# A fused attention and gated-unit kernel: later q loads, one low part on VectorE, and the last stage's attention rows split later

## The chip, the cores and the metric

The kernel runs on one core of one Trainium2 chip. The metric is the device time of one execution in microseconds (us); the time before is the median of three runs. The engines are called as the profile calls them: PE (TensorE; PEld is its weight load), DVE (VectorE), ACT (ScalarE), POOL (GpSimd) and SP (SyncE), which here only issues transfers, in the order of the program.

## The reference

Input x has 2048 rows of 448. Two branches are mixed by a gate of one number a row.

```
g = sigmoid((x * gate_w).sum(-1))
q, k, v = split(x @ wqkv)                  # 16 heads of 28
p = softmax(q @ k.T * 28 ** -0.5)          # per head, 2048 x 2048
a = concat(p @ v) @ wo
gate, up = x @ W_gate, x @ W_up            # 448 x 1792 each
b = (gate * (gate > 0) * up) @ W_down
out = g * a + (1 - g) * b
```

## The kernel before

Products are made at near full precision from split operands. An f32 matrix becomes a high part, an ACT copy rounded to the matmul's format (`act_high`), and a low part, the difference of the two (`low` on DVE, `pool_low` on POOL). A product is a sum of terms over high and low parts.

The program has three stages. The first projects x to q, k and v and writes q and k to DRAM. The second walks through 32 rounds, two per head (v = 2h and 2h + 1). The third is the output stage.

A round's order is written out by hand as a string of letters, one per small step, for all engines at once: `s` is a score block (PE, then ACT), `m` a row-maximum product for two heads ahead (PE, then DVE), `x` one product of the gate-and-up projection, `g` and `e` steps of the softmax, `P` and `Q` the products with v. PE is filled with the gate-and-up products, worked off as 56 units, one for each block of 128 hidden columns (14) and of 512 rows (4). A unit of 22 products reads one weight tile `wg`. Two such tiles exist. When a unit ends, `load_f` (line 588) refills its tile from `ws_d` in DRAM for the unit after next. The hidden block `h` goes to `h_d`, to be read back in the output stage.

In each even round, at its first score, `loads` brings K and q of the head two ahead: K as two transfers (line 167), q as one copy within SBUF (line 172) and four transfers (line 175). At the sixth score `small_things` sends the previous head's row sums to DRAM (`l_d`, line 665, after DVE's reciprocal `rq`) and reads them back spread over partitions (`rb`, line 671, which waits until `l_d` has landed). SP issues all of these in one queue, and whatever waits there holds what stands behind it.

The output stage is a list `todo`. `down(i)` is one of 56 steps of the down projection, 14 for each block of 512 rows, into four accumulators `acc`. Around it stand `fetch_w` and `split_wd` (weights `wdr`, split to `WD`: high on ACT, low on POOL), `fetch_h` and `split_d` (hidden rows `hr`, split to `hh`: high on ACT, low on DVE; three `hh` buffers, so ACT's split for step i + 2 waits for step i - 1). For each row block `fetch_o` loads the attention rows `or`, `split_o` splits them in two halves to `on` (high on ACT, low on POOL), `wout` multiplies a quarter of them by the output weights `WO` in 11 products, the last four with the low parts, and `result` joins both branches. `split_wo` splits the output weights `wor`. A table gives, for each row block, the step before which its load, its two splits and its four output products are put.

Of the kernel before, what the change touches and what calls it, by code (L numbers as in the profile page):

```python
# [84 lines left out]
def gated_mix_kernel(ctx, tc, x, wq, wo, wgu, wd, out):  # L85
# [8 lines left out]
    def f32(ap):  # L94
        return ap.bitcast(F32)
# [21 lines left out]
    def ps_x(name):  # L117
        return psum.tile([P, TB], F32, tag="x", bufs=2, name=name)
# [7 lines left out]
    def low(dst, src, high):  # L126
        nc.vector.tensor_tensor(dst, src, f32(high), op=OP.subtract)  # L127

    def pool_low(dst, src, high):
        nc.gpsimd.tensor_tensor(dst, src, f32(high), op=OP.subtract)  # L130
# [20 lines left out]
    def last_q(name, dt=F32R):  # L151
        return vp.tile([P, 4, TB], dt, name=name, tag="Q2", bufs=1)
# [11 lines left out]
    def load_k(h):  # L164
        k = qk_d[2 * DH * h:2 * DH * h + DH].rearrange("d r t -> (d r) t")
        for a in (0, 2 * DH):
            nc.sync.dma_start(f32(K[h % 3])[a:a + 2 * DH], k)

    def load_q(h):
        Q[h] = QS[h % 3].rearrange("p j t -> p (j t)")  # L170
        if h > 2:
            nc.sync.dma_start(f32(Q[h])[GD:GD + 2], f32(Q[h])[GD + 2:GD + 4])
        for a in range(2):
            for r in range(2):
                nc.sync.dma_start(f32(Q[h])[2 * DH * a + r:2 * DH * (a + 1):2], qk_d[2 * DH * h + DH:2 * DH * (h + 1), a])
# [14 lines left out]
    def smax(k):  # L190

        h, u, half = maxima[k]
        full = 4 * rows_of(h).count(2)
        if u == 0 and half == 0:
            MX[h] = keep.tile([P, 2 * full], F32, name=f"mx_{h}", tag="mx", bufs=2)
            M[h] = keep.tile([P, NU[h]], F32, name=f"m_{h}", tag="m", bufs=2)
        ps = ps_w(f"sm_{k}")
        for c in range(2):
            k0 = (half * 2 + c) * TB
            nc.tensor.matmul(ps[:, c, :], Q[h][:, u * P:(u + 1) * P], K[h % 3][:, k0:k0 + TB],  # L200
                             start=True, stop=True)
        c = 2 * u + half
        to = MX[h][:, c:c + 1] if u < full else M[h][:, u:u + 1]
        nc.vector.tensor_reduce(to, ps, axis=AX.XY, op=OP.max)  # L204
        if c == 2 * full - 1:
            nc.vector.tensor_reduce(M[h][:, :full], MX.pop(h).rearrange("p (a b) -> p a b", b=2), axis=AX.X, op=OP.max)
# [87 lines left out]
    def score():  # L294

        v, done, q, half, chunks = stream.pop(0)
        h = v // 2
        if q not in QUAD:
            QUAD[q] = p_slot(next(slots) % NP, f"P_{v}_{q[1]}_{q[2]}")
        ps = ps_w(f"s_{v}_{chunks[0][0]}_{chunks[0][1]}")  # L300
        for c, (k, j) in enumerate(chunks):
            nc.tensor.matmul(ps[:, c], K[h % 3][:, k * P:(k + 1) * P], Q[h][:, j * TB:(j + 1) * TB], start=True, stop=True)  # L302
            AT[v, k, j] = QUAD[q][:, 2 * half + c]
        dst = QUAD[q][:, 2 * half:2 * half + 2]
        if done:
            nc.scalar.activation(dst, ps, AF.Exp, scale=SCALE)  # L306
        else:
            nc.scalar.activation(dst, ps, AF.Copy, scale=-1.0)  # L308
            todo_max.append((v, chunks[0][1], dst, ps if v else None))
# [275 lines left out]
    def load_f(i):  # L585
        if NF <= i < NB * NF:
            WS[i] = fe.tile([P, 2, 7, P], F32R, name=f"wg_{i}", tag="wg", bufs=2)
            nc.sync.dma_start(f32(WS[i]), ws_d[i % NF])
# [103 lines left out]
    def early_d():  # L692

        for i in range(0, 4, 2):
            h = fe.tile([P, 2, 4, P], F32, name=f"hk_{i}", tag="wgr", bufs=2).rearrange("p s c f -> p (s c f)")
            for k in range(2):
                DR[i + k] = V[:, 0].rearrange("p k h d -> p (k h d)")[:, (i + k) * D:(i + k + 1) * D]
                HK[i + k] = h[:, k * TB:(k + 1) * TB]
                nc.sync.dma_start(DR[i + k], wd[(i + k) * P:(i + k + 1) * P])
                nc.sync.dma_start(HK[i + k], h_d[i + k])  # L700
# [13 lines left out]
    def small_things(u):  # L714

        h, q = divmod(u, 4)

        if u in (22, 38):
            g = 2 if u < 32 else 3
            nc.sync.dma_start(V[:, g % 2], v_d[g])  # L720
        if u == 1:
            gates()
        if u == 2:
            pack_wo()
        if h and q == 1:
            row_sums(h - 1)
            spread(h - 1)

    def loads(h):

        if 2 < h + 2 < H:
            load_k(h + 2)
            load_q(h + 2)

    split_f(0, act_high, pool_low, (0,))
    fetch_f(1)
    for v, order in enumerate(ROUNDS):
        small_things(2 * v)
        if v == 2 * H - 3:
            early_d()  # L740
        ns = 0
        for o in order:
            if o == "s":
                ns += 1
                if ns == 6:
                    small_things(2 * v + 1)
                if ns == 1 and v % 2 == 0:
                    loads(v // 2)
                if stream:
                    score()  # L750
            elif o == "m":
                if m < len(maxima):
                    smax(m)
                    m += 1
            elif o == "x":
                i, half, n = passes.pop(0)
                if n == 0:
                    units.append((i, half, ps_x(f"gu_{i}_{half}")))
                gu_mm(units[-1][2], i, half, n)
                if n == NT - 1:  # L760
                    i, half, ps = units.pop()
                    if half:
                        finished.add(i)
                        load_f(i + 2)
                    spill_h(i, ps) if half else relu(i, ps)
            elif o == "n":
                if v % 2 and v < 2 * H - 1:
                    smax_end(v // 2 + 1)
            elif o == "w":
                ready = -(-starts[v + 2] // NT)  # L770
                ready = min(ready + ready % 2, 2 * NF)
                while parts < ready and (parts < 4 or parts // 2 - 2 in finished):
                    split_f(parts // 2, act_high, pool_low, (parts % 2,))
                    parts += 1
                    if parts % 2 == 0:
                        fetch_f(parts // 2 + 1)
            elif o == "b":
                block_min()
            elif o == "A":
                all_max()  # L780
            elif o == "g":
                take_max()
            elif o == "N":
                if v > 1 and v % 2:
                    normalise(v // 2 - 1)
            elif o == "e":
                take_exp()
            elif o in "cf":
                rescale(v, "cf".index(o))
            elif o == "D":  # L790
                split_wd(len(early))
                early.append(o)
            elif o == "l":
                sends.pop()()
            elif o == "u":
                split_f(0, act_high, pool_low, (1,))
                QS.append(last_q("Q2"))
                for a, b in ((GD, 12), (GD + 12, 4)):
                    nc.sync.dma_start(f32(QS[2])[a:a + b].rearrange("p j t -> p (j t)"), Q[1][GD + 2:GD + 2 + b].bitcast(F32))
                load_q(2)  # L800
                fetch_f(2)
                parts = 2
            elif o in "PQ":
                pv(v, "PQ".index(o))
        rest = [k for k in todo_exp + todo_sub + todo_all if k[0] == v]
        assert not rest and v not in PO or len(stream) == max(0, 16 * (2 * H - 1 - v) - AHEAD), (v, passes, rest, len(stream) + 16 * (v + 1))
# [6 lines left out]
    WO = pf.tile([P, 7, D], F32R, name="WO")  # L813
# [7 lines left out]

    def split_wo(r):
        act_high(WO[:, 0:3], r[:, 0:3])
        pool_low(WO[:, 3:6], r[:, 0:3], WO[:, 0:3])
        act_high(WO[:, 6], r[:, 3])
        pool_low(WO[64:, 6], r[64:, 3], WO[64:, 6])

    ON, OR, GA, HH, ACC = {}, {}, {}, {}, {}

# [105 lines left out]
        todo[n:n] = new  # L935


    for tb, load, split, at in ((0, 3, (5, 6), (9, 10, 11, 12)), (1, 8, (13, 14), (16, 17, 18, 19)), (2, 21, (23, 25), (28,) * 4),
                                (3, 35, (37, 39), (42,) * 4)):
        before(load, (fetch_o, tb))  # L940
        for k, i in enumerate(split):
            before(i, (split_o, tb, 2 * k))
        for t, i in enumerate(at):
            before(i, (wout, tb, t))
# [40 lines left out]
```

## Time and profile before

| | |
|---|---|
| median of three timed runs | 1223.49 us (1223.36 to 1225.96) |
| the profiled execution | 1228.39 us, span 1226.6 us |
| mean granted PE clock | 0.994 |
| busy: PE, DVE, ACT, POOL | 1199.1, 906.3, 867.9, 753.9 us |
| transferred | 178.36 MB, 145 GB/s over the span |

The span runs from the first to the last instruction. The profile names, for each instruction, the idle time of its engine before it and what ended that time. `wg<-ws_d` means that the tile `wg` is written from `ws_d`. The first stage takes some 140 us, the rounds last until about 1030 us, and the rest is the output stage.

### The profile page before, as it was taken

How to read it: one execution, taken by the hardware profiler on the slowest of the kernel's cores; microseconds unless marked ns; L12 is line 12 of the kernel's file. 1: busy time of each engine (PE TensorE's matmuls, PEld its weight loads, DVE VectorE, ACT ScalarE, POOL GpSimd, SP SyncE). 2: the span in 40 equal slices, each digit the busy share in tenths (PEclk: the TensorE clock that was granted, in tenths of full speed). 3: DMA queues.
4: the chain of work that ended last, by engine and by line, in shares of the span. 5: the costliest groups of instructions: out<-in, count | busy, mean ns of one | idle time of the engine just before them, and what ended most of it. 6: DMA issues, size and time to landing. Idle time of an engine off the chain costs nothing.

```text
span 1226.6 us, 16848 instructions
## 1 busy us (share of the span) xinstructions
PE 1199.1 (98%) x6183; PEld 823.1 (67%) x6183; DVE 906.3 (74%) x1177; ACT 867.9 (71%) x956; POOL 753.9 (61%) x328
## 2 busy tenths in 40 slices
PE   9999999999999999999999999999999999899998
PEld 6888655565656565656665666666565656799997
DVE  6466798889898888978897989898888552443342
ACT  5322798998989888877887888888887886422121
POOL 4221588989898766666775777777666885621020
PEclk9999999999999999999999999999999999899999
DMA  9856444454445435152545344354523325633342
GB/s 329 297 197 258 146 161 135 148 168 129 141 124 184 116 143 152 52 155 78 155 134 163 112 121 129 104 143 159 152 81 117 121 86 183 182 122 119 108 134 81
DMA packets 63486, 178.36 MB, mean 145 GB/s; under 512 B 13050, under 2 KB 19650, under 8 KB 58754
## 3 DMA queue, kind: packets, MB, share of 16 engines
q1 hardware_dynamic: 56812, 151.53, 40.4%
q0 software_dynamic: 6160, 25.30, 5.3%
q8 instruction: 49, 0.80, 0.3%
q10 hardware_dynamic: 432, 0.46, 0.1%
q14 instruction: 33, 0.27, 0.1%
HBM read 118.58 MB, written 58.87 MB: 145 GB/s over the span
## 4 chain that ended last, share of the span: by engine, by line
PE 80%; DMA 7%; DVE 6%; ACT 3%; POOL 1%; issue 1%; SPq 0%; DVEq 0%; POOLq 0%; ACTq 0%
PE gu L596 17%; PE po L649 17%; PE s L302 16%; PE acc L890 10%; PE sm L200 9%; PE qk L423 5%; DMA wg<-ws_d 4%; PE wo L849 3%; PE v L441 3%; DVE mx L204 2%; DVE r L256 2%; ACT P L308 1%; DMA X<-x_d 1%; POOL P L285 1%; DMA or<-o_d 1%
## 5 line engine op out<-in xcount | busy, mean ns | idle before, releaser
L285 POOL TENSOR_TENSOR P<-P,rm 128x2048 f32<-128x2048 f32 x102 | 470.5, 4629 | 108.5 <-DVE rm L279 86.0
L596 PE MATMUL gu<-X,wg 128*128 128x512 f32 x1232 | 366.4, 397 | 9.5 <-DMA wg<-ws_d 8.7
L204 DVE TENSOR_REDUCE mx<-sm 128x1 f32<-128x1024 f32 x256 | 302.4, 1218 | 52.7 <-PE sm L200 52.4
L302 PE MATMUL s<-Q,K 128*128 128x512 f32 x1024 | 318.0, 406 | 6.1 <-ACT P L306 2.0
L596 PEld LDWEIGHTS gu<-X,wg 128*128 128x128 f32 x1232 | 231.1, 189 | 69.8 <-DMA wg<-ws_d 10.9
L302 PEld LDWEIGHTS s<-Q,K 128*128 128x128 f32 x1024 | 180.2, 188 | 98.9 <-ACT P L306 12.7
L308 ACT ACTIVATE P<-s 128x1024 f32<-128x1024 f32 x204 | 202.4, 1038 | 62.0 <-PE s L302 60.4
L649 PE MATMUL po<-P,V 128*32 128x512 f32 x1640 | 228.0, 594 | 0.7 <-ACT rl L606 0.6
L306 ACT ACTIVATE P<-s 128x1024 f32<-128x1024 f32 x206 | 198.8, 1034 | 11.3 <-PE s L302 10.1
L292 ACT ACTIVATE P<-P 128x2048 f32<-128x2048 f32 x102 | 196.4, 1933 | 1.3 <-POOL P L285 1.0
L256 DVE SCALAR_TENSOR_TENSOR r<-s,r 128x1024 f32<-128x1024 f32 x124 | 151.7, 1224 | 26.1 <-ACT P L308 14.7
L200 PE MATMUL sm<-K,Q 128*128 128x512 f32 x520 | 169.0, 407 | 1.2 <-DVE r L256 0.7
L649 PEld LDWEIGHTS po<-P,V 128*32 128x32 f32 x1640 | 64.0, 110 | 118.9 <-issue 112.1
L649 PE MATMUL po<-V 128*32 128x512 f32 x408 | 136.0, 594 | 0.0
L285 POOL TENSOR_TENSOR V<-V,rm 128x2048 f32<-128x2048 f32 x24 | 110.9, 4625 | 24.9 <-DVE rm L279 19.3
L200 PEld LDWEIGHTS sm<-K,Q 128*128 128x128 f32 x520 | 90.6, 189 | 39.8 <-ACT P L306 9.4
L127 DVE TENSOR_TENSOR hh<-hr,hh 128x512 fp32r<-128x512 f32 x52 | 52.1, 1009 | 87.8 <-ACT hh L121 87.8
L121 ACT ACTIVATE hh<-hr 128x512 fp32r<-128x512 f32 x52 | 32.8, 631 | 115.4 <-PE acc L890 115.2
L890 PE MATMUL acc<-WD,hh 128*128 128x448 f32 x480 | 102.7, 373 | 4.9 <-ACT hh L121 3.7
L890 PEld LDWEIGHTS acc<-WD,hh 128*128 128x128 f32 x480 | 91.3, 191 | 14.6 <-ACT hh L121 4.1
L256 DVE SCALAR_TENSOR_TENSOR r<-s,P 128x1024 f32<-128x1024 f32 x50 | 61.1, 1222 | 42.0 <-ACT P L308 41.7
L271 DVE TRANSPOSE_TENSOR_REDUCE mn<-r 128x32 f32<-128x1024 f32 x63 | 78.1, 1239 | 1.3
(87 smaller groups left out, 1141.9 us busy)
## 6 DMA issues: line engine op xcount, KB each, us to landing
wg<-ws_d SPq DMA_DIRECT2D x42, 896.0 KB
K<-qk_d SPq DMA_DIRECT2D x32, 448.0 KB
Q<-qk_d SPq DMA_DIRECT2D x64, 224.0 KB
h_d<-h SPq DMA_DIRECT2D x56, 256.0 KB
hr<-h_d SPq DMA_DIRECT2D x52, 256.0 KB
ws_d<-wg SPq DMA_DIRECT2D x14, 896.0 KB
qk_d<-st POOLq DMA_DIRECT2D x21, 512.0 KB, 3.1
wgr<-wgu SPq DMA_DIRECT2D x13, 512.0 KB
```

What stands on the lines that cost most here:

```text
L200: nc.tensor.matmul(ps[:, c, :], Q[h][:, u * P:(u + 1) * P], K[h % 3][:, k0:k0 + TB], start=True, stop=True)
L204: nc.vector.tensor_reduce(to, ps, axis=AX.XY, op=OP.max)
L256: nc.vector.scalar_tensor_tensor(r, ps, -1.0, before, op0=OP.mult, op1=OP.min)
L271: nc.vector.tensor_reduce(MN[:, 1:3], R2.pop((v, j)).rearrange("p a (b r) -> p a b r", r=32), axis=AX.X, op=OP.min, apply_transpose=True)
L285: nc.gpsimd.tensor_tensor(QUAD[q], QUAD[q], m, op=OP.subtract)
L292: nc.scalar.activation(q, q, AF.Exp, scale=-SCALE)
L302: nc.tensor.matmul(ps[:, c], K[h % 3][:, k * P:(k + 1) * P], Q[h][:, j * TB:(j + 1) * TB], start=True, stop=True)
L306: nc.scalar.activation(dst, ps, AF.Exp, scale=SCALE)
L308: nc.scalar.activation(dst, ps, AF.Copy, scale=-1.0)
L596: nc.tensor.matmul(ps, WS[i][:, s, a], xf(i // NF, b), start=(n == 0), stop=(n == NT - 1))
L649: nc.tensor.matmul(po[32 * j:32 * j + 32], V[:, h // 4 % 2, k, h % 4], AT.pop((v, k, j)), start=(k == k0), stop=(k == k0 + NK // 2 - 1))
L890: nc.tensor.matmul(ACC[i // NF][t][:, :D], HH[i][:, a, t * P:(t + 1) * P], wd_high_low(f, b), start=(f == 0 and n == 0), stop=(f == NF - 1 ...
```

## The change

Three edits. `loads` takes the loader to call: K is still loaded at the first score of an even round, and q now at the ninth. The low part of the output weights is made on DVE (`low`) and not on POOL (`pool_low`). In the table of the output stage the first two row blocks have their load, splits and output products one to two steps of `down` later.

```
-    def loads(h):
+    def loads(h, load):
 
         if 2 < h + 2 < H:
-            load_k(h + 2)
-            load_q(h + 2)
+            load(h + 2)
...
-                if ns == 1 and v % 2 == 0:
-                    loads(v // 2)
+                if ns in (1, 9) and v % 2 == 0:
+                    loads(v // 2, load_k if ns == 1 else load_q)
...
     def split_wo(r):
         act_high(WO[:, 0:3], r[:, 0:3])
-        pool_low(WO[:, 3:6], r[:, 0:3], WO[:, 0:3])
+        low(WO[:, 3:6], r[:, 0:3], WO[:, 0:3])
         act_high(WO[:, 6], r[:, 3])
-        pool_low(WO[64:, 6], r[64:, 3], WO[64:, 6])
+        low(WO[64:, 6], r[64:, 3], WO[64:, 6])
...
-    for tb, load, split, at in ((0, 3, (5, 6), (9, 10, 11, 12)), (1, 8, (13, 14), (16, 17, 18, 19)), (2, 21, (23, 25), (28,) * 4),
+    for tb, load, split, at in ((0, 4, (7, 8), (10, 11, 12, 13)), (1, 10, (15, 16), (18, 19, 20, 21)), (2, 21, (23, 25), (28,) * 4),
                                 (3, 35, (37, 39), (42,) * 4)):
```

SP's queue in an even round, before (`ls` is the row sum of the head just finished):

```order
L659 DMA ls_3571<-os_3318 128x1x16
L167 DMA K_103<-qk_d 56x2048 x2
L172 DMA Q_106<-Q_106 2x2048
L175 DMA Q_106<-qk_d 28x2048 x4
L588 DMA wg_3598<-ws_d_1316 128x1792
L615 DMA h_d_3602<-h_3600 128x512
L665 DMA l_d_84<-rq_3651 128x16
L671 DMA rb_3654<-l_d_84 32x512 x4
L588 DMA wg_3698<-ws_d_1525 128x1792
```

The same round after the change:

```order
L659 DMA ls_3571<-os_3318 128x1x16
L167 DMA K_103<-qk_d 56x2048 x2
L588 DMA wg_3593<-ws_d_1316 128x1792
L615 DMA h_d_3597<-h_3595 128x512
L665 DMA l_d_84<-rq_3646 128x16
L671 DMA rb_3649<-l_d_84 32x512 x4
L172 DMA Q_106<-Q_106 2x2048
L175 DMA Q_106<-qk_d 28x2048 x4
L588 DMA wg_3698<-ws_d_1525 128x1792
```

The five q issues moved past one refill of `wg`, one store of `h` and the five issues of the row sums, and stand now right ahead of the second refill.

ACT's queue at the start of the output stage, before, from the third split after `WO`:

```order
L121 ACTIVATE hh_9048<-hr_8884 128x512
L121 ACTIVATE WD<-wdr_8922 128x448
L121 ACTIVATE hh_9069<-hr_8928 128x512
L121 ACTIVATE on_0_9074<-or_9028 128x1024
L121 ACTIVATE WD<-wdr_8926 128x448
L121 ACTIVATE hh_9094<-hr_9005 128x512
L121 ACTIVATE on_0_9074<-or_9028 128x1024
```

And after:

```order
L121 ACTIVATE hh_9044<-hr_8884 128x512
L121 ACTIVATE WD<-wdr_8922 128x448
L121 ACTIVATE hh_9069<-hr_8928 128x512
L121 ACTIVATE WD<-wdr_8926 128x448
L121 ACTIVATE hh_9090<-hr_9005 128x512
L121 ACTIVATE WD<-wdr_9021 128x448
L121 ACTIVATE hh_9109<-hr_9026 128x512
L121 ACTIVATE on_0_9114<-or_9049 128x1024
L121 ACTIVATE WD<-wdr_9042 128x448
L121 ACTIVATE hh_9132<-hr_9047 128x512
L121 ACTIVATE on_0_9114<-or_9049 128x1024
```

The first copy of the attention rows stands behind two more splits of weights and two more of hidden rows (`hh` of steps 8 and 9).

POOL's queue there, before (`os` times `rb` is the last head's normalisation):

```order
L675 TENSOR_TENSOR os_8658<-os_8658,rb_8915 128x512
L130 TENSOR_TENSOR WO<-wor,WO 128x1344
L130 TENSOR_TENSOR WO<-wor,WO 64x448
L130 TENSOR_TENSOR WD<-wdr_8876,WD 128x448
L130 TENSOR_TENSOR WD<-wdr_8878,WD 128x448
```

DVE's after the change, from the splits of steps 2 and 3 on:

```order
L127 TENSOR_TENSOR hh_8959<-hk_8222,hh_8959 128x512
L127 TENSOR_TENSOR hh_8978<-hk_8222,hh_8978 128x512
L127 TENSOR_TENSOR WO<-wor,WO 128x1344
L127 TENSOR_TENSOR WO<-wor,WO 64x448
L127 TENSOR_TENSOR hh_9002<-hr_8861,hh_9002 128x512
L127 TENSOR_TENSOR hh_9023<-hr_8865,hh_9023 128x512
```

The two instructions on `WO` left POOL, where the weights' low parts now follow the normalisation directly, and stand on DVE ahead of the low part of step 4's hidden rows.

## The prediction

> **What bounds the kernel now.** I began with the page: PE is busy 98% of the span and the chain that ended last is 80% PE, so time can only come from the stretches in which PE waits, or runs at a lower clock. The waits of PE alone, for the rounds from 400 to 900 us, name nearly one thing:
>
> ```profile
> PE gu L596 <- DMA wg<-ws_d: 8.7, 5, 2.6
> ```
>
> Five times in this kernel PE waits for a gate-and-up weight tile, 8.7 us in all, 2.6 at most. Next I asked for busy time and granted clock in stretches around such waits (columns: stretch, its length, busy time of PE, PEld, DVE, ACT, POOL, clock, DMA share, GB/s):
>
> ```profile
> 442.00:535.00 93.00, 93.00 (x493) 60.17 (x492) 83.52 (x111) 79.99 (x79) 67.78 (x22) 1.00 0.41 115
> 535.90:538.10 2.20, 0.07 (x2) 0.06 (x1) 0.81 (x1) 2.15 (x2) 2.20 (x2) 1.00 0.57 214
> 538.50:541.80 3.30, 3.30 (x10) 2.52 (x9) 1.94 (x2) 0.27 (x1) 3.30 (x1) 0.50 0.39 88
> 654.60:657.90 3.30, 3.30 (x10) 2.56 (x9) 1.86 (x2) 0.00 (x0) 3.30 (x1) 0.50 0.33 86
> 1064.20:1070.90 6.70, 5.54 (x16) 4.56 (x15) 6.17 (x4) 3.90 (x8) 6.70 (x4) 0.50 0.37 113
> ```
>
> Between two waits PE is busy 93.00 of 93 us: nothing else holds it there. The second row is one wait; the third shows that PE then ran 3.3 us at half clock, and the fourth shows the same after another wait. The last is the output stage, 5.54 busy us at half clock. Half-clock work takes twice its time, so these cost 1.65, 1.65 and 2.8 us on top of the waits.
>
> **Why the weight tile is late.** SP's queue in head 5's round, and PE there:
>
> ```profile
> 409.83 0.87 SPq L167 DMA_DIRECT2D K<-qk_d  x2
> 410.76 0.66 SPq L172 DMA_DIRECT2D Q<-Q  x1
> 411.47 3.15 SPq L175 DMA_DIRECT2D Q<-qk_d  x4
> 414.72 0.48 SPq L588 DMA_DIRECT2D wg<-ws_d  x1
> ...
> 425.05 1.72 SPq L671 DMA_DIRECT2D rb<-l_d  x4
> 426.87 0.37 SPq L588 DMA_DIRECT2D wg<-ws_d  x1
> ```
>
> ```profile
> 409.71 0.85 PE L596 MATMUL gu<-X,wg 128*128 128x512 f32 x3
> ...
> 421.61 0.62 PE L302 MATMUL s<-Q,K 128*128 128x512 f32 x2
> 424.19 0.50 PE L596 MATMUL gu<-X,wg 128*128 128x512 f32 x1 [1.96 <-DMA wg<-ws_d]
> ...
> 442.88 0.62 PE L596 MATMUL gu<-X,wg 128*128 128x512 f32 x2
> ...
> 447.27 0.69 PE L200 MATMUL sm<-K,Q 128*128 128x512 f32 x2
> ```
>
> The tile that PE frees at 410.56 (409.71 + 0.85) could be refilled from then on, but SP issues K and five q transfers first and reaches the refill at 414.72. It lands when PE resumes, 9.5 us later, 1.96 us late.
>
> **The change part by part.** *q behind the row sums.* K's two issues end at 410.70 (409.83 + 0.87), so the refill goes out at about 410.8, 3.9 us earlier. With the landing time unchanged at 9.5 us it is there at 420.3, and PE wanted it at 422.23 (424.19 less 1.96). I take no credit for q's bytes no longer being ahead of it; that makes 1.9 us of slack a lower bound. The longest of the five waits is 2.6 us, under 3.9, so all five go: 8.7 us, and the half clock behind two of them, 1.65 + 1.65. Together 12.0.
>
> The five q issues (0.66 + 3.15 = 3.8 us) now stand between rb, whose issue ends at 426.77, and the next refill, which went out at 426.87. That refill moves to about 430.7 with q's bytes before it, the same case as the old one: 9.5 us later is 440.2. Its tile is first used at 442.88, about 2 us earlier in the new schedule, so at 440.9. It just fits, and I price it at 0 with up to 1 us at each of five places if rb goes out no earlier. I expect rb earlier, since it waits for a small write that queues behind q's bytes today. What reads the new q first is the row maximum at 447.27, over 14 us after q's last issue even with PE 2 us earlier; there is no wait there. The q copy waits for nothing new: the last scores of the head that held its slot are done by the first score of the round. Behind it stand only SP's own later DMAs. In the other eight of thirteen heads PE waits for no refill; one of them lies in the stretch of 93.00 busy us. They gain nothing.
>
> *The output stage.* PE, ACT, SP, POOL and DVE there, and the group of DVE's splits over the kernel:
>
> ```profile
> 1050.14 9.89 PE L890 MATMUL acc<-WD,hh 128*128 128x448 f32 x48
> 1063.78 0.84 PE L890 MATMUL acc<-WD,hh 128*128 128x448 f32 x2 [3.74 <-ACT hh L121]
> 1065.78 4.10 PE L890 MATMUL acc<-WD,hh 128*128 128x448 f32 x10 [1.16 <-DVE hh L127]
> ```
>
> ```profile
> 1043.58 1.78 ACT L121 ACTIVATE WO<-wor 128x1344 fp32r<-128x1344 f32 x2
> ...
> 1052.77 0.63 ACT L121 ACTIVATE hh<-hr 128x512 fp32r<-128x512 f32 x1 [1.33 <-PE acc L890]
> 1061.68 1.06 ACT L121 ACTIVATE on<-or 128x1024 fp32r<-128x1024 f32 x1 [8.28 <-DMA or<-o_d]
> ```
>
> ```profile
> 1053.04 0.36 SPq L873 DMA_DIRECT2D wdr<-wd  x1
> 1053.49 0.38 SPq L879 DMA_DIRECT2D hr<-h_d  x1
> 1053.92 0.42 SPq L833 DMA_DIRECT2D or<-o_d  x1
> ```
>
> ```profile
> 1046.34 5.12 POOL L130 TENSOR_TENSOR WO<-wor,WO 128x1344 fp32r<-128x1344 f32 x2
> 1051.53 4.16 POOL L130 TENSOR_TENSOR WD<-wdr,WD 128x448 fp32r<-128x448 f32 x3
> 1062.82 2.36 POOL L130 TENSOR_TENSOR on<-or,on 128x1024 fp32r<-128x1024 f32 x1 [7.12 <-ACT on L121]
> 1065.13 1.59 POOL L130 TENSOR_TENSOR WD<-wdr,WD 128x448 fp32r<-128x448 f32 x1
> 1066.69 2.82 POOL L130 TENSOR_TENSOR on<-or,on 128x1024 fp32r<-128x1024 f32 x1
> ```
>
> ```profile
> L127 DVE TENSOR_TENSOR hh<-hr,hh 128x512 fp32r<-128x512 f32 x52 | 52.1, 1009 | 87.8 <-ACT hh L121 87.8
> ```
>
> ```profile
> 1048.57 1.86 DVE L127 TENSOR_TENSOR hh<-hr,hh 128x512 fp32r<-128x512 f32 x1 [1.65 <-ACT hh L121]
> ...
> 1063.76 6.29 DVE L127 TENSOR_TENSOR hh<-hr,hh 128x512 fp32r<-128x512 f32 x3 [9.08 <-ACT hh L121]
> ```
>
> ACT takes its work in order. Its copy of the attention rows waits 8.28 us for them, the hidden splits behind it are late, and PE loses 3.74 + 1.16 us and 2.8 to half clock: 7.7 us. The rows are late because SP stood before a wdr load until POOL had done WO's low part and the WD split behind it.
>
> After the change POOL is spared the 5.12 us, and ACT meets the copy two steps later, with the splits of steps 8 and 9 already issued. A step of the down projection is 9.89 / 4 = 2.47 us; step 4 starts at 1050.14, so step 10, with the first output product before it, is due at 1065.0. The rows' load stands behind one more wdr and hr, which the emptier POOL lets go sooner; its issue I leave at 1053.9. Before, it landed 7.8 us after (1061.68 less 1053.92) with two loads issued in the 0.9 us ahead of it and more behind. I estimate 6 us, so 1060, with 1061.7 as the late end. ACT's first copy then ends at 1061.0, and POOL's two low parts with a WD between them take 2.36 + 1.59 + 2.82 = 6.8 from there: 1067.8. PE reads the last half at the tenth of 11 output products, each of the size of acc's (9.89 / 48 = 0.206), so at 1065.0 + 9 x 0.206 = 1066.8. By these POOL durations the wait is 1.0, by the shorter 2.36 for both 0.6; I take 1.0. With the late landing it is 2.7, with an early one nothing. The stage so gives 7.7 less 1.0: 6.7 us.
>
> *WO's low part on DVE.* It is 1344 + 448 columns against 512 of a split with a mean of 1.009 us: 3.5 us. The three splits of 6.29 us, run beside POOL, give 2.1 each and 7.3 us for WO; the low end lies within the cover. It can start at about 1044.9, when ACT's first WO copy is done (1344 of 1792 columns of the 1.78 us from 1043.58); behind it on DVE stands the low part of step 4, needed at 1050.14 plus two products, so at about 1050.5. With 3.5 + 1.0 it is there at 1049.4, hidden by steps 1 to 3 of PE; with 7.3 + 2.1 at 1054.3, a wait of 3.8 us and perhaps a half-clock stretch of 1.7. I take 0, nearer the mean row since POOL is no longer full there.
>
> A rule speaks against this part. By the row, one split took 1.86 us while POOL worked on WO, against a mean of 1.009. The Trainium skill, "SBUF — State Buffer", section "SBUF: two separate sides", says that a DVE instruction with two inputs in SBUF and a GpSimd instruction that reads SBUF lock each other out for the whole instruction. By that rule moving WO frees POOL's queue but not the shared path, and the cost is nearer the upper end. The row agrees in direction.
>
> *The sum.* 12.0 + 6.7 = 18.7 us. The profiled execution took 1228.4 (span 1226.6 and 1.8 around it), so 1209.7. The median of the timed runs is 1223.5, 4.9 less. Without its 6.1 us of half clock the profiled one would be 1222.3, so I read the gap mostly as fewer half-clock stretches in timed runs, which the change would remove anyway: 1222.3 - 8.7 - (3.74 + 1.16 - 1.0) is 1209.7 again. If instead profiling itself adds 4.9 us, the timed result is 1204.8.
>
> On the half clock: a wait of 2.13 us (row 535.90, 2.20 less 0.07 busy) was enough here. The Trainium skill, "TensorE: Matmul & The Clock Gate", section "HAM oscillation — how this bites in real kernels", puts the harm at idle gaps over about 3.4 us; the trace disagrees for the waits on weights. By the rule alone the sum would lose their 3.3 us and come to 1213.0.
>
> **The rivals.** *The output stage gives it back*: DVE's WO delays step 4, or POOL's last low part makes PE wait and drop its clock. For it speaks that both have under 2 us of slack. The rounds' 12.0 us stay: 1228.4 - 12.0 = 1216.4. Chance 0.17. *The refill stays late*, because the landing and not the issue is slow, and the wait moves to the second refill behind q. Against it: 3.9 us of earlier issue against 2.6 of wait. Only the output stage gains, 1228.4 - 6.7 = 1221.7. Chance 0.08. *The edit does less than it says*: freed from the weights, rounds wait for DVE (83.52 of 93 busy) instead and win back half, 1228.4 - 6.0 - 6.7 = 1215.7. Chance 0.06. *Slower*: q lands after PE wants the row maxima, in each of 13 heads (one q copy each). It decides if q lands over 14 us after its last issue at 430.7. Waits of 2 us with a half-clock stretch of 1.7 each cost 13 x 3.7 = 48, 1228.4 - 18.7 + 48 = 1257.7. Against it stand the 9.5 us that the landing of the refill took behind the same bytes. Chance 0.04.
>
> **How the numbers follow.** My forecast keeps 0.65. Its own range goes from 1203 (profiling adds the gap, no wait in the output stage) to 1213. The range to quote takes in the first and third rival and the upper bounds of DVE and POOL (1209.7 + 5.5 + 1.7 = 1216.9): 1203 to 1217. About 0.2% (2.4 us) is what a measurement of this kernel can tell from no change. Forecast, first and third rival, and most of the second are faster by more: 0.94; same 0.02; slower 0.04.
>
> **What would show it.** Right: no wait of PE for wg; the refill issued within 1 us of K, q after rb; no half clock between 442 and 900; ACT's wait for the rows near 2 us instead of 8.28. Wrong: waits of PE for wg at the second refill, for q at the row maxima, or at steps 4 and 10 of the last stage.

## The result, and the profile after

| | before | after |
|---|---|---|
| timed runs, median | 1223.52 us (1223.36 to 1225.96) | 1208.28 us (1206.50 to 1211.96) |
| ratio | | 0.9875 [0.9848, 0.9901] |
| the profiled execution | 1228.39 us, span 1226.6 | 1206.50 us, span 1204.7 |
| mean granted PE clock in it | 0.994 | 0.999 |

Run again with five rounds the changed kernel took 1207.51 us against 1226.23 of before in the same rounds, 0.985 [0.9836, 0.9864]. One of the eleven runs of before there was slow, 1658.46 us at a granted clock of 0.654; it is in that median and left out of the ratio. The forecast of 1209.7 us and its range held.

The rounds from 400 to 900 us, as busy time and clock (columns as in the prediction):

```profile
400.00:900.00 500.00, 500.00 (x2713) 318.53 (x2712) 439.41 (x579) 426.74 (x418) 358.14 (x109) 1.00 0.43 129
```

PE is busy all 500 us at full clock; before, it was busy for 491.10 of them. SP's queue in head 5's round:

```profile
408.98 0.60 SPq L659 DMA_DIRECT2D ls<-os  x1
409.68 0.87 SPq L167 DMA_DIRECT2D K<-qk_d  x2
410.64 0.34 SPq L588 DMA_DIRECT2D wg<-ws_d  x1
411.23 0.37 SPq L615 DMA_DIRECT2D h_d<-h  x1
419.45 0.32 SPq L665 DMA_DIRECT2D l_d<-rq  x1
420.89 1.71 SPq L671 DMA_DIRECT2D rb<-l_d  x4
422.64 0.65 SPq L172 DMA_DIRECT2D Q<-Q  x1
423.33 3.15 SPq L175 DMA_DIRECT2D Q<-qk_d  x4
426.59 0.47 SPq L588 DMA_DIRECT2D wg<-ws_d  x1
```

The refill follows K at once. `rb` goes out 1.4 us after `l_d` (419.45 to 420.89), so that the second refill, behind q, is issued at 426.59, no later than before. PE uses the two tiles without a wait:

```profile
421.97 0.40 PE L596 MATMUL gu<-X,wg 128*128 128x512 f32 x1
```

```profile
440.52 0.63 PE L596 MATMUL gu<-X,wg 128*128 128x512 f32 x2
```

The output stage, on PE, ACT, SP, POOL and DVE:

```profile
1051.83 2.02 PE L848 MATMUL wo<-WO,on 128*128 128x448 f32 x9
1054.54 0.67 PE L848 MATMUL wo<-WO,on 128*128 128x448 f32 x2 [0.69 <-POOL on L130]
```

```profile
1046.58 1.06 ACT L121 ACTIVATE on<-or 128x1024 fp32r<-128x1024 f32 x1 [1.36 <-DMA or<-o_d]
```

```profile
1039.53 0.42 SPq L832 DMA_DIRECT2D or<-o_d  x1
```

```profile
1047.72 2.42 POOL L130 TENSOR_TENSOR on<-or,on 128x1024 fp32r<-128x1024 f32 x1 [3.25 <-ACT on L121]
1050.09 1.61 POOL L130 TENSOR_TENSOR WD<-wdr,WD 128x448 fp32r<-128x448 f32 x1
1051.67 2.82 POOL L130 TENSOR_TENSOR on<-or,on 128x1024 fp32r<-128x1024 f32 x1
```

```profile
1031.35 4.15 DVE L127 TENSOR_TENSOR WO<-wor,WO 128x1344 fp32r<-128x1344 f32 x2 [0.52 <-ACT WO L121]
```

ACT waits 1.36 us for the attention rows instead of 8.28. PE stops once, for 0.69 us after nine of eleven output products, for POOL's second low part: the wait that the prediction put at 1.0. WO's low part took DVE 4.15 us.

### The profile page after: what moved, and what is told of

Read it like the earlier page. It is cut to its first block, busy times and chain, and to the rows that moved or that the text cites. A ratio compares the mean times of both kernels' runs of the same rounds, so it can differ in the third digit from the quotient of the medians.

```text
span 1204.7 us, 16835 instructions
## 1 busy us (share of the span) xinstructions
PE 1190.6 (99%) x6183; PEld 821.9 (68%) x6183; DVE 905.7 (75%) x1179; ACT 867.6 (72%) x956; POOL 750.1 (62%) x326
## 4 chain that ended last, share of the span: by engine, by line
PE 82%; DVE 9%; ACT 3%; DMA 3%; issue 2%; POOL 1%; SPq 0%; DVEq 0%; ACTq 0%; POOLq 0%
PE gu L596 18%; PE po L649 18%; PE s L302 17%; PE sm L200 10%; PE acc L889 8%; PE qk L423 6%; DVE mx L204 3%; PE wo L848 3%; PE v L441 3%; DVE r L256 2%; ACT P L308 2%; DMA or<-o_d 1%; DMA h_d<-h 1%; POOL P L285 1%; DVE mn L271 1%
## 5 line engine op out<-in xcount | busy, mean ns | idle before, releaser
L127 DVE TENSOR_TENSOR hh<-hr,hh 128x512 fp32r<-128x512 f32 x52 | 48.0, 933 | 79.3 <-ACT hh L121 79.3
L889 PE MATMUL acc<-WD,hh 128*128 128x448 f32 x480 | 99.9, 366 | 0.2
```

The lines of the kernel that those rows point to most:

```text
L889: nc.tensor.matmul(ACC[i // NF][t][:, :D], HH[i][:, a, t * P:(t + 1) * P], wd_high_low(f, b), start=(f == 0 and n == 0), stop=(f == NF - 1 ...
```

## The experiments

The theory has two halves: in the rounds, q ahead of the refill makes the refill late; in the output stage, POOL's work on WO and ACT's order make the hidden splits late. The first four runs take the change apart.

**q alone.** Only the edits of `loads`.

> Only q moves to the ninth score; output stage as before. My theory (SP's issue slots held the refill back): the five waits of PE for wg (8.7 us) go, and the two half-clock stretches behind them; the output stage keeps its two waits of 3.7 and 1.2 us. Timed 1223.5 - 8.7 to - 12.0, so 1211.5 to 1215. Rival (the waits go elsewhere in the rounds, to DVE or to the second refill): 1218 or more. Rival (the output stage carries the gain): within 2 us of 1223.5.

1213.60 us against 1225.39, ratio 0.9909 [0.9887, 0.9931], inside the range of my theory. PE is busy 500.00 of the 500 us from 400 to 900, and what it waits for most is now the output stage:

```profile
PE acc L889 <- ACT hh L121: 4.3, 1, 4.3
```

So q accounts for the whole gain in the rounds. The output stage keeps its waits, 4.3 and 0.9 us.

**WO alone.**

```
-        pool_low(WO[:, 3:6], r[:, 0:3], WO[:, 0:3])
+        low(WO[:, 3:6], r[:, 0:3], WO[:, 0:3])
```

(and the same for the second part)

> Only WO's low part moves to DVE. The rows' load then goes out about 1.7 us earlier (nearer 1052.2 than 1053.9) and lands 6 to 7 us later, at about 1059; ACT's wait falls from 8.28 to about 6, and PE's wait before step 8 from 3.74 + 1.16 to 2 to 3.5 in all. Timed 1219.5 to 1222. Rival (WO on POOL was the whole cause): wait under 0.5, 1216 to 1218. Rival (DVE's lock delays step 4): a wait of PE at step 4 of up to 3.8, 1223 to 1229.

1219.54 us against 1225.39, 0.9960 [0.9945, 0.9974]. ACT's wait for the rows, and the waits of PE:

```profile
1053.14 1.06 ACT L121 ACTIVATE on<-or 128x1024 fp32r<-128x1024 f32 x1 [4.73 <-DMA or<-o_d]
```

```profile
PE gu L596 <- DMA wg<-ws_d: 6.7, 5, 2.0
...
PE acc L890 <- DVE hh L127: 1.6, 2, 1.3
...
PE acc L890 <- ACT hh L121: 0.2, 1, 0.2
```

ACT still stands before the rows, but 4.73 us and not 8.28. PE's waits in the stage fall from 4.9 to 1.8 us, a little better than I had expected, and step 4 didn't wait: the rival in which DVE is locked out falls. The waits for `wg`, which this edit leaves alone, came to 6.7 us here and to 8.7 before: their size differs from one execution to the next.

**The table alone.**

> Only the table moves. POOL still makes WO's low part, so the load goes out later, at about 1055, and lands near 1062; ACT's copy no longer stands before the splits of steps 8 and 9, so the wait before step 8 goes, but POOL's second low part ends at about 1070 against 1066.8: a wait of about 3.4 in the output products, with half clock behind it. Timed 1219 to 1222. Rival (ACT's order was the whole cause): no wait over 1 us, 1216 to 1218.

1223.53 us against 1225.39, 0.9989 [0.9974, 1.0004]: no difference that can be told.

```profile
PE wo L849 <- POOL on L130: 3.5, 1, 3.5
PE wo L849 <- ACT on L121: 1.9, 2, 1.0
```

The wait before step 8 has gone and comes back as 5.4 us in the output products: 3.5 for POOL, as expected (3.4), and 1.9 for ACT's copies, which I had not seen. The time came out 3.0 us above the middle of my range; 1.9 of these are the kernel before, which took 1225.39 us here and 1223.5 when I set the range.

**WO and table.**

> WO and table, q as before. The five waits for wg stay at about 8.7 us with their half clock; the output stage is as after the change: one wait of 0.7 us. Timed 1223.5 - 4.1 to - 6.9, so 1216.5 to 1219.5, and with q's gain from the run on q alone it should add up to the whole change within 2 us. Rival (the parts depend on each other): the sum misses by more.

1218.28 us against 1225.39, 0.9949 [0.9931, 0.9966]. PE's waits:

```profile
PE gu L596 <- DMA wg<-ws_d: 8.7, 5, 2.4
PE wo L849 <- POOL on L130: 2.1, 1, 2.1
```

The stage's two edits are worth 0.51%, q 0.91%; together 1.42%, against 1.25% and 1.50% in the two measurements of the whole. The parts add, within what the intervals can tell. The wait for POOL was 2.1 us here, where I had expected 0.7 as in the first trace. It goes with the landing of the rows: ACT waited 2.67 us for them here and 1.36 in the first trace.

Next, why the refill was late. The prediction spoke of SP's issue slots, 3.9 us of them, and left the landing time unchanged. Another cause moves with q just as well: its bytes, which lie ahead of the refill's on the transfer engines.

**Half of q's bytes, the same issues.** The kernel before, with half of each q row from head 3 on:

```
+        n = S // 2 if h > 2 else S
...
-                nc.sync.dma_start(f32(Q[h])[2 * DH * a + r:2 * DH * (a + 1):2], qk_d[...])
+                nc.sync.dma_start(f32(Q[h])[2 * DH * a + r:2 * DH * (a + 1):2, :n], qk_d[..., :n])
```

> The kernel before, but each q transfer from head 3 on brings half its columns (the other half of the slot keeps an older head's values): the same number of issues at the same places, half of q's bytes. Theory A (the issue slots hold the refill, bytes count little): refill still issued 4.15 us after its unit, lands about 0.6 us sooner, five or four waits of 5 to 6.5 us in all; about 3 us faster than before. Theory B (q's bytes ahead of the refill on the transfer engines hold it): it lands 2 us sooner, waits of 1 us in all, no half clock behind them; 8 to 11 us faster, nearly what moving q brings.

1213.93 us against 1226.23, 0.9899 [0.9882, 0.9916]. This kernel leaves out half of q, so it serves for timing alone. SP and PE in head 5's round:

```profile
409.92 0.87 SPq L167 DMA_DIRECT2D K<-qk_d  x2
410.85 0.66 SPq L172 DMA_DIRECT2D Q<-Q  x1
411.55 3.16 SPq L176 DMA_DIRECT2D Q<-qk_d  x4
414.81 0.48 SPq L589 DMA_DIRECT2D wg<-ws_d  x1
```

```profile
422.21 0.39 PE L597 MATMUL gu<-X,wg 128*128 128x512 f32 x1
```

The refill goes out as late as before, at 414.81, and PE doesn't wait: theory B. Leaving out half of the bytes brings as much as moving q does (1.01% here, 0.91% with q alone).

**The issues without the bytes.** The changed kernel with five small transfers between K and the refill:

```
             load(h + 2)
+            if load is load_k:
+                s = keep.tile([2 * DH, 5, 4], F32, name=f"few_{h}", tag="few", bufs=2)
+                for k in range(5):
+                    nc.sync.dma_start(s[:DH, k], qk_d[..., 0, 4 * k:4 * k + 4])
```

> The changed kernel with five small transfers (28 rows of 16 bytes, read by nobody) between K and the refill: q's issue slots without its bytes. If the slots alone hold the refill, it goes out about 4 us after its unit as before the change, and lands 9 us later, 1 to 2.6 us late at four or five places: 5 to 10 us slower than the changed kernel. If the bytes matter as the half-q run showed (landing in 9.0 us with all of q, 6.0 with half), it lands in 4.8 to 5.5 us after its issue, about 420 in the first of the five rounds against 422.2: no wait, same time as the changed kernel.

1208.28 us against 1225.31, 0.9864 [0.9826, 0.9902]; the changed kernel had 0.985 against its own before, no difference that can be told. The slots took 2.29 us and not 3.8, so this run does not bring the refill's issue back to where it was before the change:

```profile
411.11 2.29 SPq L736 DMA_DIRECT2D few<-qk_d  x5
413.50 0.34 SPq L588 DMA_DIRECT2D wg<-ws_d  x1
```

The records of the transfer packets (128 packets of 7168 bytes a tile) show when the refill had landed. From K's issue, mean of the five late refills:

| kernel | refill issued after K's issue, us | landed after K's issue, us |
|---|---|---|
| before | 4.9 | 13.7 |
| half of q's bytes | 4.9 | 10.9 |
| change, with five small transfers | 3.2 | 8.9 |
| change | 1.0 | 8.6 |

Half of q's bytes is worth 2.7 us. Issuing 2.2 us earlier is worth 0.3. What is missing is a refill issued as late as before, with none of q's bytes ahead of it. The traces have it already, in the four even rounds between the five (heads 6, 8, 10 and 12). There PE frees the tile only 4.8 us after K, so the refill goes out late with the change too. Head 6's round before, the same after, and SP's wait for PE in it after:

```profile
467.81 0.92 SPq L167 DMA_DIRECT2D K<-qk_d  x2
...
472.74 0.48 SPq L588 DMA_DIRECT2D wg<-ws_d  x1
```

```profile
465.42 0.92 SPq L167 DMA_DIRECT2D K<-qk_d  x2
470.21 0.34 SPq L588 DMA_DIRECT2D wg<-ws_d  x1
```

```profile
SPq L588 <- PE gu L596: 3.8, 1, 3.8
```

In these four rounds the refill is issued 4.9 us after K before the change and 4.8 after it, and by the same packet records it lands 13.5 us after K before and 9.6 after. So of the 5.0 us by which the five late refills land earlier, about 4 are q's bytes, and the issue slots are worth 1 us at most. The Trainium skill, "DMA: Bandwidth & Descriptors", section "Queues, rings and completion order", says that each transfer engine takes the descriptors of one queue in order; the table agrees.

**q on another queue.** The kernel before, with q issued on ACT's queue (`nc.scalar.dma_start`) from head 3 on.

> The kernel before, but q from head 3 on is issued on ACT's queue at the first score: its bytes at the old time, SP's slots free. The refill goes out within 1 us of K. If slots count, it lands at most 9 us later, no wait for wg: 8 to 11 us faster in the rounds, less what five issues a head cost ACT. If the bytes count, it lands 10 to 12 us after its issue, about when it did before less 1 to 3 us: waits of 0 to 1.5 us at the five places, or none but with ACT late (waits of PE for P, ACT).

1245.42 us against 1225.31, 1.0169 [1.0135, 1.0204]. It doesn't decide between slots and bytes, since ACT did not wait for the end of the previous head as SP does and issued q some 8 us ahead of K. The waits for `wg` went, but ACT paid:

```profile
185.10 8.44 ACTq L176 DMA_DIRECT2D Q<-qk_d  x3
193.65 1.94 ACT L309 ACTIVATE P<-s 128x1024 f32<-128x1024 f32 x2 [8.24 <-DMA Q<-qk_d]
```

```profile
PE s L303 <- ACT P L309: 10.3, 3, 3.6
PE s L303 <- ACT V L309: 2.8, 1, 2.8
```

In four rounds before 400 us ACT sat before a q transfer and PE waited 2.8 to 3.6 us each time.

**q ahead of the row sums.** The changed kernel with 5 in place of 9: q still passes the refill, but not `l_d` and `rb`.

> q at the fifth score: behind the refill of wg, but ahead of the row sums again. My theory (all that counts is that the refill goes out ahead of q): no wait of PE for wg, refill issued within 1 us of K, time within 1.5 us of the changed kernel. Rival (passing the row sums counts too, by what waits for rb on POOL or by the second refill behind q): 2 us or more slower than the changed kernel, with waits of PE for wg at the second refill.

1209.83 us (1209.63 to 1211.51) against 1226.23, 0.9870 [0.9853, 0.9886]; the changed kernel in the same rounds had 1207.51 (1207.20 to 1208.99), 0.9850 [0.9836, 0.9864]. The intervals of the ratios overlap, but the two sets of runs don't, and the 2.3 us between the medians are more than the 1.5 that my theory allowed. The time is the rival's; the waits that it named are not there. PE has no wait for `wg`, and the refill and `rb` in the traced round are:

```profile
410.86 0.34 SPq L588 DMA_DIRECT2D wg<-ws_d  x1
...
423.98 1.72 SPq L671 DMA_DIRECT2D rb<-l_d  x4
425.80 0.37 SPq L588 DMA_DIRECT2D wg<-ws_d  x1
```

`rb` goes out 3 us later than in the changed kernel, and no wait of PE in the rounds comes from it. At step 4 of the output stage this trace is 0.24 us behind the changed kernel's second trace, at the end 4.4. So the difference arose in the output stage: a wait of 2.12 us for POOL with half clock behind it (last section), against 1.56 and none in the changed kernel, and a slower pace of PE after it. The edit doesn't touch that stage; whether it brings these is not shown. In the rounds, passing the refill is what counts.

**The output products one step later.** The one wait left in the stage is POOL's second low part. The changed kernel with

```
-((0, 4, (7, 8), (10, 11, 12, 13)),
+((0, 4, (7, 8), (11, 12, 13, 13)),
```

> The changed kernel with the first row block's output products one more step later (11, 12, 13, 13). The wait for POOL's second low part (0.69 to 2.1 us) has 2.4 us of cover and goes; 0.5 to 2 us faster than the changed kernel, at the edge of what can be told. Rival (results of step 13 come late, since two output products stand right ahead of it, and the next accumulators wait for DVE): a new wait of PE at step 14, no faster.

> The changed kernel once more, for the comparisons of this round: about 0.9875 of before, with one wait of PE of 0.5 to 2.2 us for POOL's second low part in the first output product (0.69 in the first trace, 2.12 in the run with WO and table alone).

1205.87 us (1204.93 to 1206.64), 0.9834 [0.9820, 0.9848], against 1207.51 (1207.20 to 1208.99) of the changed kernel in the same rounds; the two sets of five runs don't overlap. The waits of PE in the changed kernel's second trace, from 1020 us on:

```profile
PE wo L848 <- POOL on L130: 1.6, 1, 1.6
```

With the products later the same answer is empty, and there is no wait at step 14 either: the rival falls. The gain of 1.6 us is inside the 0.5 to 2 expected. This is the fastest of the versions run, at the edge of what can be told.

## Why the prediction was right, and where it was not

*The rounds.* Forecast 12.0 us. In the traces step 4 of the output stage starts at 1050.14 before and follows here:

```profile
1036.57 15.42 PE L889 MATMUL acc<-WD,hh 128*128 128x448 f32 x72
```

That is 13.6 us. All five waits went, with both half-clock stretches. The excess comes in small part from what a wait costs beyond its shown idle: at the first of the five, PE came 2.22 us earlier (424.19 to 421.97), 0.11 of them from before the wait, for 1.96 of idle. The rest is open. There is luck in the 12.0, too: in the traces of WO alone, table alone and both, which leave the rounds as they were, the same waits came to 6.7, 7.8 and 8.7 us, and I had priced one trace.

*The mechanism in the rounds was wrong.* The step that failed is "With the landing time unchanged at 9.5 us" and the 3.9 us of issue slots before it. With the issue as late as before but none of q's bytes ahead, the refill landed 3.9 us earlier (13.5 to 9.6 after K); the slots added 1 us at most. So mainly q's bytes held the refill. The result was right because both move with q, and because the slack that I called a lower bound was one: in head 5's round the packets had landed at 418.4 and PE used the tile at 421.97. The rival "the refill stays late, because the landing and not the issue is slow" had the right cause and the wrong end: the landing was slow by reason of the very transfer that was moved. An edit that freed the slots and left the bytes ahead of the refill would, by the table, have won little, though no run shows it; the same argument would have forecast a gain for it.

*Behind q.* I priced the second refill at 430.7, just in time. It went out at 426.59, since `l_d` no longer queued behind q's bytes: `rb` followed it after 1.4 us and not 5.5. The sentence that expected this was right, and the 0 too. The row maxima didn't wait, so the rival "slower" fell.

*The output stage.* Forecast 6.7 us, measured 21.9 - 13.6 = 8.3. The load went out 2.96 us after step 4's start (forecast 3.8), landed 7.05 us later (6), and POOL then needed 6.77 us (6.8). The wait came to 0.69, 1.56, 2.1 and 2.3 us in the traces with WO and table, so the forecast of 1.0 is inside what varies, on its low side. (With 2.36 for both low parts the prediction's own sum gives 0.5, not 0.6.) DVE's 4.15 us for WO lie between the mean row's 3.5 and the contended 7.3; the next splits were in time. Some 2.0 us of the 8.3 were not in the sum: before the change PE ran the rest of the stage slightly slower, from about 1092 us on, some 20 us behind the stall. The last 168 products, before and after, in the chain of waits:

```profile
1188.21 34.73 PE acc L890 x168
```

```profile
1166.91 34.06 PE acc L889 x168
```

That is 0.67 us a block of 14 steps, over three blocks. Nothing shows that the change brings it: these products took 34.06 us with the table alone, too, 34.73 with q alone, and with q at the fifth score the pace changed within the stage. Those 2.0 us are luck as far as is known; without them the stage gave 6.3 us, against 6.7 forecast.

*Profile against timed runs.* I read the gap of 4.9 us mostly as half-clock stretches and not as a cost of profiling. The profiled execution of the changed kernel was the fastest of its four, which speaks against a fixed cost of profiling. But the runs don't bear out the half-clock reading either. Of the 27 runs of before that stand beside q alone, 17 had a granted clock of 0.993 or 0.994, as the profiled one had, and took 1224.0 to 1228.4 us with a median of 1225.5. So with as much half clock an execution is in the middle 2.9 us faster than the profiled one, and more than half of the gap was scatter whose cause stays open. That 1209.7 lies so near to 1208.28 is in part luck.

## What to carry to other kernels

When a wait ends on a transfer, look not only at when it was issued but at what lies ahead of it on the transfer engines; a bulk load that is not needed soon belongs behind one that is. Halving the bytes, and issuing without bytes, tell the two apart in two runs; a round in which the transfer goes out late anyway can tell it from the traces at hand. Two edits in one stage may each be worth little alone when each only moves the wait to the other's engine: table alone nothing that can be told, WO alone 0.4%, and the wait that is left says where the next step goes.

## What the runs showed of the hardware

In the output stage PE has two paces that the granted clock doesn't show: with no wait in between, a product of 128x448 starts every 34.06 / 168 = 0.203 us or every 34.73 / 168 = 0.207 us, both at clock 1.00. A trace keeps one pace for tens of us. In the trace of the changed kernel it changes where PE stops; in that of before it changes at about 1092 us with no stop there. What sets it stays open.

A wait of 2.12 us in the output stage was followed by half clock in one run (q at the fifth score) and not in another (WO and table). The rows behind it:

```profile
1056.70:1059.90 3.20, 3.20 (x11) 2.82 (x10) 0.00 (x0) 0.00 (x0) 1.93 (x2) 0.50 0.72 224
```

```profile
1069.10:1073.00 3.90, 3.90 (x20) 3.62 (x21) 0.59 (x2) 0.63 (x1) 2.54 (x2) 1.00 0.62 201
```

Nor does the longer wait always bring it. In the trace of the table alone a wait of 2.25 us for `wg` was followed by full clock, one of 1.99 us by half:

```profile
425.50:429.00 3.50, 3.50 (x16) 2.75 (x16) 3.01 (x3) 1.73 (x3) 3.50 (x1) 1.00 0.32 85
539.60:542.90 3.30, 3.30 (x10) 2.53 (x9) 2.45 (x2) 0.71 (x1) 3.30 (x1) 0.50 0.56 114
```

The granted clock in the trace of before changes only in whole steps: a half-clock stretch in the rounds is 3.41 us long, and the full-clock stretches between the changes, 112.64, 406.19 and 157.01 us, are 33, 119 and 46 times that.

The Trainium skill, "TensorE: Matmul & The Clock Gate", section "What's actually happening", says that activity is judged in windows that run freely from the kernel. These cases agree with that, though no run tests it. If it is the cause, the price of a wait near 2 us is a chance and not a number.
